# The first four token tiles taken one by one through w1, with w1 loaded in quarters

## The chip, the cores and the metric

The kernel runs on one core of one Trainium2 chip. The metric is device time in microseconds (us): the median of several executions. The record lists the span and the mean granted clock of every run (the granted clock is the share of TensorE's full clock that the profile shows as granted: 1.00 from 28.0 to 31.4 us before the change, 0.50 there after it), and of each kernel one execution's whole trace is kept. In the profile PE is TensorE, PEld its weight loads, DVE VectorE, ACT ScalarE, POOL GpSimd, and SP the engine that issues most DMAs. Times of lines in a trace count from the start of the span, which is about 2 us shorter than the device time (1514.3 against 1516.2 us before the change).

Ratios are the mean time of one kernel's fast runs over that of the other's fast runs of the same rounds, so they are not quite the ratios of the medians quoted here.

## The reference

```python
def reference(A_x, ..., B_w1, B_w2, B_w3, B_w4):        # cut
    def _B_ref(x, w1, w2, w3, w4):
        h = _gelu(_layernorm(x, axis=-1) @ w1)          # <- the stage that was changed
        ... four shifts of h along the tokens ...
        hs = concatenate([g0, g1, g2, g3], axis=-1) @ w2
        x1 = x + hs
        return x1 + _gelu(_layernorm(x1, axis=-1) @ w3) @ w4
    x = A_x                                             # 2048 tokens x 1024, bf16
    xn = _layernorm(x, axis=-1)
    return x + _A_ref(xn, ...) + _B_ref(xn, ...)        # _A_ref: attention by segments of 32 tokens
```

There are 2048 tokens in 16 tiles of 128. w1 is 1024 x 1024; the kernel holds it as 8 slices of 128 rows, the slices of the contraction. Only the first 5% of the kernel's time is at stake here: layernorm, w1 and gelu.

## The kernel before

Each tile is loaded, its mean and variance are taken (VectorE, with a power on GpSimd), it is normalised into `xn2` (VectorE), transposed so that features lie on partitions (by TensorE for tiles 0 to 3, by DMA for the others), multiplied by w1 (TensorE) and put through gelu (ScalarE). Beside this, ScalarE normalises `x` itself in place (`normalise_x`), and TensorE then adds it up by segments (`seg_sums`) for the attention. In the timelines below ScalarE works through its queue in the order in which the program issues (before the change four normalisations from 24.53 us, and the gelus behind them from 29.07).

```python
load_x(0); load_x(1); load_w1(0)            # w1 in two halves of four slices
load_x(2); load_x(3); load_w1(4)
for n in range(4, 8): load_x(n)
...
warm(16)                                     # useless matmuls, 0.427 us apart until the granted clock became 1.0 at 7.03 us
ln_stats(0); ln_stats(1)
ln_apply(0); pe_trans(0); warm(2)
ln_apply(1); pe_trans(1)
normalise_x(0); normalise_x(1)
... (cut: PSUM for the first pair)
for co in range(KT): w1_first(co, range(4))  # tiles 0 and 1 together: 256 columns a matmul
... (cut: statistics of tiles 2 to 5)
for c0 in range(0, KT, 2):
    w1_first(c0, range(4, KT)); w1_first(c0 + 1, range(4, KT)); w1_first_out((c0, c0 + 1))
    if c0 in (0, 2): pe_trans(c0 // 2 + 2)
for g in range(1, NT // 2):                  # the other seven pairs
    ... (cut: statistics and DMA transposes of the next pair)
    stage1(g, range(4))
    if g == 1:
        seg_sums(0); seg_sums(1)
        normalise_x(2); normalise_x(3)
    for n in nxt: normalise_x(n)             # with g == 1: tiles 4 and 5
    stage1(g, range(4, KT))
    seg_sums(2 * g); seg_sums(2 * g + 1)     # wait for normalise_x of these tiles
```

I call two tiles taken together a pair; the third pair is tiles 4 and 5. A `psX` line in a trace is a segment sum.

## Time and profile before

| | before |
|---|---|
| device time, median of 6 | 1516.2 us (1516.06 to 1516.35) |
| TensorE busy, of a span of 1514.3 us | 1497.6 us |
| first w1 matmul | 10.72 us |
| third pair starts | 29.48 us |
| w2 starts | 73.81 us |
| last matmul ends, to end of span | 3.80 us |

Two lines of the page's first and fourth part: the busy time of each engine, then each engine's share of the chain of work that ended last.

```profile
PE 1497.6 (99%) x9456; PEld 793.3 (52%) x9582; DVE 660.3 (44%) x1553; ACT 452.8 (30%) x1251; POOL 235.0 (16%) x652
...
PE 95%; DVE 3%; ACT 1%; issue 1%; DMA 0%; DVEq 0%; ACTq 0%
```

TensorE is the limit nearly everywhere. What can be gained in the first stage is therefore the time in which TensorE has no useful work there. The timeline of TensorE before shows it. The columns are start, length of the group, engine, source line, operation, output<-inputs, shape and count; in brackets is the idle time before the group and what ended it.

```profile
1.47 6.36 PE L197 MATMUL psW<-fill 128*128 128x512 bf16 x16 [1.47 <-DVE fill L175]
7.91 0.62 PE L243 MATMUL psT<-c_ident_sb,xn 128*128 128x128 bf16 x8
8.36 0.59 PE L197 MATMUL psW<-fill 128*128 128x512 bf16 x2
9.54 0.62 PE L243 MATMUL psT<-c_ident_sb,xn 128*128 128x128 bf16 x8 [0.58 <-DVE xn L218]
10.72 4.71 PE L285 MATMUL ps<-xn2T,w_sb 128*128 128x256 bf16 x40 [0.56 <-DVE xn2T L246]
...
19.50 1.03 PE L285 MATMUL ps<-xn2T,w_sb 128*128 128x256 bf16 x8 [0.96 <-ACT hT_all L290]
20.37 3.66 PE L258 MATMUL ps<-xn2T,w_sb 128*128 128x256 bf16 x32
...
27.75 0.54 PE L253 MATMUL psX<-c_segone_sb,x 128*128 128x4 bf16 x16
29.48 7.15 PE L258 MATMUL ps<-xn2T,w_sb 128*128 128x256 bf16 x64 [1.19 <-ACT hT_all L260]
```

Useful work begins at 10.72 us, because the first pair needs two tiles normalised, transposed and copied. Small holes follow, the last one before the third pair. From 29.48 us on TensorE never waits until w2 at 73.81. So the place to watch is the start of the third pair: what moves it moves the whole kernel. ScalarE's timeline shows why that last hole is there:

```profile
24.53 4.63 ACT L235 ACTIVATE x<-x,nm,lnst 128x1024 bf16<-128x1024 bf16 x4
29.07 1.17 ACT L260 ACTIVATE hT_all<-ps 128x256 bf16<-128x256 f32 x4
```

Four normalisations stand in ScalarE's queue ahead of gelus. TensorE's wait of 1.19 us before the third pair ended with the output of such a gelu (`hT_all`, L260), which reads the PSUM tile that TensorE wrote its sums to.

### The profile page before, as it was taken

What the parts mean: (1) busy time and instruction counts of PE and PEld (TensorE: products, weight loads), DVE (VectorE), ACT (ScalarE), POOL (GpSimd) and SP (SyncE); (2) the same over time, 40 slices, a digit from 0 to 9 for tenths busy, and PEclk for the clock granted to TensorE, in tenths of its full rate; (3) what the DMA queues carried; (4) which work ended last, traced back from release to release, by engine and by line L of the source; (5) the groups of instructions that cost most, each with busy time, mean ns of one, the idle gap of its engine ahead of it and who ended that gap; (6) DMA issues with size and microseconds to landing.
All of it is one profiled execution on the core that took longest, in us unless ns stands there. A gap on an engine that the chain in (4) does not pass through costs nothing.

```text
span 1514.3 us, 23917 instructions
## 1 busy us (share of the span) xinstructions
PE 1497.6 (99%) x9456; PEld 793.3 (52%) x9582; DVE 660.3 (44%) x1553; ACT 452.8 (30%) x1251; POOL 235.0 (16%) x652
## 2 busy tenths in 40 slices
PE   8999999999999999999999999999999999999998
PEld 6844444444444466666544554444444544454446
DVE  8284010010110226666622857731767640676653
ACT  5633202103012034454401344310433420334320
POOL 4142110111110211121210111110111110111100
PEclk9999999999999999999999999999999999999999
DMA  7699553553122545574522454421464431344211
GB/s 199 158 246 291 218 188 98 180 173 135 63 91 46 191 151 170 157 206 141 180 70 82 140 167 140 154 87 52 138 169 144 140 117 56 118 140 140 94 36 38
DMA packets 191029, 208.38 MB, mean 138 GB/s; under 512 B 51192, under 2 KB 158856, under 8 KB 190912
## 3 DMA queue, kind: packets, MB, share of 16 engines
q1 hardware_dynamic: 183664, 182.49, 40.2%
q0 software_dynamic: 7248, 24.31, 4.1%
q8 instruction: 77, 1.26, 0.4%
q14 instruction: 40, 0.33, 0.1%
HBM read 170.07 MB, written 25.17 MB: 129 GB/s over the span
## 4 chain that ended last, share of the span: by engine, by line
PE 95%; DVE 3%; ACT 1%; issue 1%; DMA 0%; DVEq 0%; ACTq 0%
PE psP L754 15%; PE psQ L582 14%; PE psK L598 14%; PE psV L605 14%; PE ps L517 13%; PE ps L535 13%; PE ps L339 4%; PE ps L258 3%; PE psO L657 2%; PE psS L627 2%; PE psM L614 1%; PE psY L776 1%; PE psvb L399 1%; PE psG L408 1%; PE ps L285 0%
## 5 line engine op out<-in xcount | busy, mean ns | idle before, releaser
L754 PE MATMUL psP<-wo_sb,oX 128*128 128x512 bf16 (+1 forms) x1036 | 221.7, 372 | 1.1
L631 ACT ACTIVATE ET<-psS 32x132 f32<-32x132 f32 x512 | 138.7, 271 | 188.8 <-PE psS L627 183.1
L535 PE MATMUL ps<-w,hT_all 128*128 128x512 bf16 x874 | 193.7, 379 | 1.2
L598 PE MATMUL psK<-xT,w 128*128 128x512 bf16 x747 | 176.3, 379 | 1.1
L582 PE MATMUL psQ<-xT,w 128*128 128x512 bf16 x750 | 175.9, 379 | 1.1
L605 PE MATMUL psV<-w,xT 128*128 128x512 bf16 x745 | 175.0, 379 | 1.0
L598 PEld LDWEIGHTS <-w 128*128 128x128 bf16 x1280 | 121.3, 98 | 80.1
L754 PEld LDWEIGHTS <-oX 128*128 128x128 bf16 x1056 | 102.8, 98 | 115.5
L582 PEld LDWEIGHTS <-w 128*128 128x128 bf16 x1024 | 96.9, 98 | 105.4 <-issue 1.3
L518 ACT ACTIVATE hT_all<-ps 128x512 bf16<-128x512 f32 x112 | 66.7, 597 | 283.9 <-PE ps L517 283.9
L535 PEld LDWEIGHTS <-hT_all 128*128 128x128 bf16 x896 | 87.0, 98 | 103.9
L665 ACT CAST oTm<-psO 128x16 bf16<-128x16 f32 x128 | 22.9, 179 | 366.1 <-DVE oX L661 366.1
L633 DVE STREAM_TRANSPOSE EQ<-ET 128x128 f32<-128x128 f32 x128 | 39.8, 311 | 165.6 <-ACT ET L631 165.2
L589 DVE TENSOR_TENSOR Q<-psQ,QM 128x512 bf16<-128x512 f32 (+1 forms) x128 | 85.2, 678 | 61.4 <-ACT Q L588 43.2
L605 PEld LDWEIGHTS <-xT 128*128 128x128 bf16 x768 | 72.1, 98 | 73.4
L648 POOL TENSOR_TENSOR BD<-ET,c_segone_sb 128x16 bf16<-128x16 f32 x128 | 33.7, 263 | 491.8 <-ACT ET L631 491.8
L517 PE MATMUL ps<-xn3T,w3a 128*128 128x512 bf16 x448 | 97.7, 379 | 0.0
L517 PE MATMUL ps<-xn3T,w3b 128*128 128x512 bf16 x448 | 97.7, 379 | 0.0
L646 DVE TENSOR_TENSOR BD<-PT,c_segone_sb 128x512 bf16<-128x512 bf16 x128 | 90.0, 703 | 4.4
L760 DVE TENSOR_TENSOR ot<-psP,Rt 128x512 bf16<-128x512 f32 (+1 forms) x33 | 22.2, 674 | 155.4 <-PE psP L754 155.4
L661 DVE TENSOR_TENSOR oX<-psO,VM 128x512 bf16<-128x512 f32 (+1 forms) x128 | 86.3, 674 | 7.2 <-PE psO L657 7.2
L599 ACT CAST K<-psK 128x512 bf16<-128x512 f32 (+1 forms) x160 | 78.5, 506 | 33.0 <-PE psK L598 32.4
(157 smaller groups left out, 1541.5 us busy)
## 6 DMA issues: line engine op xcount, KB each, us to landing
w<-in_A_Wq_dram SPq DMA_DIRECT2D x32, 1024.0 KB, 5.7
w<-in_A_Wk_dram SPq DMA_DIRECT2D x32, 1024.0 KB, 5.7
w<-in_A_Wv_dram SPq DMA_DIRECT2D x32, 1024.0 KB, 5.7
R_scratch<-x POOLq DMA_DIRECT2D x16, 512.0 KB, 4.1
R<-R_scratch SPq DMA_DIRECT2D x16, 512.0 KB, 7.8
chunk<-in_A_Wv_dram SPq DMA_DIRECT2D x8, 1024.0 KB, 6.3
R_scratch<-R POOLq DMA_DIRECT2D x16, 512.0 KB, 6.2
chunk<-in_A_Wo_dram SPq DMA_DIRECT2D x8, 1024.0 KB, 6.2
```

The costliest lines, as they stand in the source:

```text
L517: nc.tensor.matmul(ps[:], w3[:, k, (f % FH) * P:(f % FH + 1) * P], xn3Ts[tb][:, :, k, :], start=(k == 0), stop=(k == KT - 1))
L518: nc.scalar.activation(h3T[:, f, :], ps[:], ACTF.Gelu_apprx_tanh)
L535: nc.tensor.matmul(ps[:], h3T[:, f, j * P:(j + 1) * P], w4t[f // 4][:, f % 4, ch * 512:(ch + 1) * 512], start=(f == 0), stop=(f == FT - 1))
L582: nc.tensor.matmul(ps[:], w[:, k, hh * P:(hh + 1) * P], s.xm[:, k, 0:512], start=(k == 0), stop=(k == KT - 1))
L589: nc.vector.tensor_tensor(q3[:, j0:16, 0:SEG], p3_[:, j0:16, :], QM[:, 4 * s.hg + hh, z + j0:z + 16].unsqueeze(2).to_broadcast((P, 16 - j0 ...
L598: nc.tensor.matmul(ps[:, 0:c], w[:, k, hh * P:(hh + 1) * P], s.xm[:, k, h2 * c:(h2 + 1) * c], start=(k == 0), stop=(k == KT - 1))
L599: nc.scalar.copy(s.K[:, hh, h2 * c:(h2 + 1) * c], ps[:, 0:c])
L605: nc.tensor.matmul(ps[:], s.xm[:, k, m * P:(m + 1) * P], w[:, k, :], start=(k == 0), stop=(k == KT - 1))
L631: nc.scalar.activation(ET[q, :, :], ps[q, :, W * j:W * (j + 1)], ACTF.Exp, scale=SCALE)
L646: nc.vector.tensor_tensor(B4[:, :, :, 0:SEG], PT[:].unsqueeze(2).to_broadcast((P, 4, 4, SEG)), so.unsqueeze(3).to_broadcast((P, 4, 4, SEG) ...
L661: nc.vector.tensor_tensor(oX[:, hsl(s.hg), m * P:(m + 1) * P].rearrange("p h (j i) -> p h j i", i=SEG)[:, :, j0:4, :], p4[:, :, j0:4, 0:SE ...
L754: nc.tensor.matmul(ps[:, 0:w], oX[:, h, m * P:(m + 1) * P], wo_sb[:, h, cc], start=(h == 0), stop=(h == H - 1))
```

## The change

The intent: start w1 as soon as one tile and the first slices of w1 are there, and fill the early holes. w1 comes in four loads of two slices. Tile 0 runs with the slices outermost, so each slice is used as it lands. Tiles 0 to 3 go one at a time, with 128 columns a matmul. The statistics of tiles 1 and 2 are taken in halves around the normalisation of the tile before. All copies of transposed tiles go to ScalarE. The loop over pairs starts at the third.

```diff
             def load_w1(k0):
-                nc.sync.dma_start(w1_sb[:, k0:k0 + 4, :], w1_v[:, k0:k0 + 4, :])
+                nc.sync.dma_start(w1_sb[:, k0:k0 + 2, :], w1_v[:, k0:k0 + 2, :])
             load_x(0)
             load_x(1)
             load_w1(0)
+            load_w1(2)
             load_x(2)
-            load_x(3)
             load_w1(4)
-            for n in range(4, 8):
+            load_w1(6)
+            for n in range(3, 8):
                 load_x(n)
# ... cut: ln_half, and the copies of pe_trans all to ScalarE
-            warm(16)
+            warm(12)
             ln_stats(0)
-            ln_stats(1)
+            ln_half(1, 0)
             ln_apply(0)
             pe_trans(0)
-            warm(2)
+            ln_half(1, 1)
+            w1_first(range(5))
+            ln_half(2, 0)
             ln_apply(1)
             pe_trans(1)
# ... cut: the first pair's code, removed
+            w1_first(range(5, KT))
+            for b in range(2):
+                gelu4(0, b, first[:, b, :, :])
+            ln_half(2, 1)
+            ln_apply(2)
+            single(1, 0)
+            pe_trans(2)
+            normalise_x(0)
+            single(1, 1)
+            ln_stats(3)
+            ln_stats(4)
+            ln_apply(3)
+            single(2, 0)
+            pe_trans(3)
+            normalise_x(1)
+            single(2, 1)
+            ln_stats(5)
+            ln_apply(4)
+            dma_trans(4)
+            single(3, 0)
+            seg_sums(0)
+            seg_sums(1)
+            ln_stats(6)
+            ln_apply(5)
+            dma_trans(5)
+            single(3, 1)
+            for n in range(2, 6):
+                normalise_x(n)
+            seg_sums(2)
+            seg_sums(3)
-            for g in range(1, NT // 2):
+            for g in range(2, NT // 2):
# ... cut
```

`single(n, b)` is one tile's product with one half of w1's columns: 32 matmuls of 128 columns.

More of the change, by code (lines that the diff above doesn't have):

```diff
@@ L197, in warm, with ln_half @@
                     nc.tensor.matmul(ps[:], fill[:, 0:P], fill[:], start=(i == 0), stop=(i == c - 1))
-            def ln_stats(n):
-                st = ring.tile([P, 2, 6], F32, tag="st")
-                for c in range(2):
-                    nc.vector.bn_stats(st[:, c, :], xts[n][:, c * 512:(c + 1) * 512])
-                nc.vector.bn_aggr(lnst[:, n, 0:2], st[:])
-                ab = ring.tile([P, 2], F32, tag="ab")
+            sts = {}
+            def ln_half(n, c):
+                if c == 0:
+                    sts[n] = ring.tile([P, 2, 6], F32, tag="st", name="st")
+                nc.vector.bn_stats(sts[n][:, c, :], xts[n][:, c * 512:(c + 1) * 512])
+                if c == 0:
+                    return
+                nc.vector.bn_aggr(lnst[:, n, 0:2], sts.pop(n)[:])
+                ab = ring.tile([P, 2], F32, tag="ab", name="ab")
                 nc.vector.tensor_scalar(ab[:, 0:1], lnst[:, n, 1:2], EPS, None, op0=ALU.add)
@@ L207, in ln_stats @@
                 nc.gpsimd.tensor_tensor(lnst[:, n, 2:4], ab[:], neghalf[:], op=ALU.pow)
+            def ln_stats(n):
+                ln_half(n, 0)
+                ln_half(n, 1)
             xn2Ts = {}
@@ L243, in pe_trans @@
                         nc.tensor.matmul(p3_[:, k, :], xn2[:, (4 * h + k) * P:(4 * h + k + 1) * P], ident[:], start=True, stop=True)
-                    dst = xn2Ts[n // 2][:, n % 2, 4 * h:4 * h + 4, :]
-                    if h == 0 and n < 2:
-                        nc.vector.tensor_copy(dst, p3_)
-                    else:
-                        nc.scalar.copy(dst, p3_)
+                    for q in range(0, 4, 2 if n == 0 else 4):
+                        w = 2 if n == 0 else 4
+                        nc.scalar.copy(xn2Ts[n // 2][:, n % 2, 4 * h + q:4 * h + q + w, :], p3_[:, q:q + w, :])
             def seg_sums(n):
@@ L264, in stage1, with w1_first @@
                     w1_part(g, co, mm_tile("ps1")[:, 0:256], range(KT))
-            warm(16)
+            first = aux_tile([P, 2, 512], "B", "ps1")[:].rearrange("p b (c t) -> p b c t", c=4)
+            def w1_first(ks):
+                for k in ks:
+                    for co in range(KT):
+                        nc.tensor.matmul(first[:, co // 4, co % 4, :], w1_sb[:, k, co * P:(co + 1) * P], xn2Ts[0][:, 0, k, :],
+                                         start=(k == 0 and co % 4 == 0), stop=(k == KT - 1), skip_group_check=True)
@@ new lines, in gelu4, with single @@
+            def gelu4(n, b, ps):
+                nc.scalar.activation(hTB[:, 4 * b:4 * b + 4, 2 + n * P:2 + n * P + P], ps, ACTF.Gelu_apprx_tanh)
+            def single(n, b):
+                ps = mm_tile("ps1")[:].rearrange("p (c t) -> p c t", c=4)
+                for c in range(4):
+                    co = 4 * b + c
+                    for k in range(KT):
+                        nc.tensor.matmul(ps[:, c, :], w1_sb[:, k, co * P:(co + 1) * P], xn2Ts[n // 2][:, n % 2, k, :], start=(k == 0), stop=(k == KT - 1))
+                gelu4(n, b, ps)
@@ L267 @@
+            warm(12)
             ln_stats(0)
-            ln_stats(1)
+            ln_half(1, 0)
             ln_apply(0)
             pe_trans(0)
-            warm(2)
+            ln_half(1, 1)
+            w1_first(range(5))
+            load_segone()
+            load_eye9()
+            ln_half(2, 0)
             ln_apply(1)
             pe_trans(1)
-            normalise_x(0)
-            normalise_x(1)
-            load_segone()
-            load_eye9()
-            first = []
-            for tag in "AB":
-                t = aux_tile([P, 2, 512], tag, "ps1")
-                first += [t[:, c // 2, (c % 2) * 256:(c % 2 + 1) * 256] for c in range(4)]
@@ L283, in w1_first @@
-            def w1_first(co, ks):
-                for k in ks:
-                    nc.tensor.matmul(first[co], w1_sb[:, k, co * P:(co + 1) * P], xn2Ts[0][:, :, k, :], start=(k == 0 and co % 2 == 0),
-                                     stop=(k == KT - 1), skip_group_check=True)
-            def w1_first_out(c):
-                for co in c:
-                    nc.scalar.activation(hTB[:, co, 2:258], first[co], ACTF.Gelu_apprx_tanh)
-            for co in range(KT):
-                w1_first(co, range(4))
@@ L294 @@
-            ln_stats(2)
-            ln_stats(3)
-            for n in (2, 3):
-                ln_apply(n)
-            ln_stats(4)
-            ln_stats(5)
-            for c0 in range(0, KT, 2):
-                w1_first(c0, range(4, KT))
-                w1_first(c0 + 1, range(4, KT))
-                w1_first_out((c0, c0 + 1))
-                if c0 in (0, 2):
-                    pe_trans(c0 // 2 + 2)
-            for g in range(1, NT // 2):
+            w1_first(range(5, KT))
+            for b in range(2):
+                gelu4(0, b, first[:, b, :, :])
@@ L307 @@
+            ln_apply(5)
[6 more added lines that the diff above has]
+            for g in range(2, NT // 2):
                 nxt = [n for n in (2 * g + 2, 2 * g + 3) if n < NT]
                 for n in nxt:
-                    if 5 < n + 1 < NT:
+                    if 6 < n + 1 < NT:
                         ln_stats(n + 1)
@@ L313 @@
                 stage1(g, range(4))
-                if g == 1:
-                    seg_sums(0)
-                    seg_sums(1)
-                    normalise_x(2)
-                    normalise_x(3)
                 for n in nxt:
```

## The prediction

> **What bounds the kernel.** TensorE: 1497.6 of 1514.3 us busy, 95% of the chain of waits. The change touches only the first stage (layernorm, transposition, w1, gelu). In the TensorE timeline w1 starts at 10.72 us; the third pair starts at 29.48 us and from there it runs unbroken to w2 at 73.81. So the time moves as the start of the third pair (tiles 4 and 5), now 29.48 us, moves.
>
> **Before, up to 29.48.** 10.72 us lead-in; 128 matmuls of 256 columns at 0.109 us start to start = 14.0; transposes of tiles 2 and 3 (0.45 each) and four segment sums (0.2 each), 1.7; holes of 3.1: about 0.3 for the second half of w1, 0.4 and 1.1 for ScalarE evacuations, and 1.2 before the third pair, where ScalarE runs four normalisations (4.6 us) ahead of gelus.
>
> **What the change does.**
> 1. Statistics split: VectorE normalises tile 0 at about 6.5 instead of 7.31; transposes at 7.1 instead of 7.9.
> 2. Tile 0 no longer waits for tile 1, and w1 comes in quarters. The landings show the first half of w1 complete between 6.9 us (fastest DMA engine) and 10.22 (slowest), and about 0.68 us per 256 KB. Estimate for the slowest engine: quarters at 8.9, 10.2, 12.2 and 13.6 us. So w1 starts near 8.9, 1.8 us earlier, but waits about 0.5 and 1.1 us for quarters two and three; tile 0 is done near 14.6.
> 3. 256 matmuls of 128 columns replace 128 of 256. Transposes of that width run 0.056 us start to start, with weight loads hidden, so +0.4 us in all. [...]
> 4. Tiles 1 to 3: from 14.6, six halves of 1.8, two transposes and two segment sums: near 26.7.
> 5. Then a new hole: the gelu of tile 3's second half (0.5) and normalisations of tiles 2 and 3 (1.18 each) run on ScalarE in order before the segment sums of tiles 2 and 3, which TensorE must do before the third pair. About 3.2 us, against 1.2 before. The third pair starts near 30.
>
> **Sum.** -1.8 (start) +0.4 (narrow matmuls) +0.45 (one more transposition after the start) +1.7 (holes 4.8 instead of 3.1) = +0.7 us. Shaded, since the quarters may land earlier. Predicted 1516.5 us, 80% range 1514.3 to 1518.3. Chances: faster by over 2% 0.01, within 2% 0.98, slower 0.01.
>
> **What would show it.** w1 starting at 8.5 to 9.2 us, with DMA of w1 ending the idle time; DMA waits inside tile 0; narrow matmuls 0.056 us apart; a hole near 3 us before the segment sums of tiles 2 and 3, ended by ScalarE's normalisation; the third pair at 29 to 31 us; 44.3 us more to w2.
>
> **What would make it wrong.** (a) Landing: if quarters arrive a microsecond earlier, tiles 0 to 3 move up and time falls to about 1515. (b) The clock. The granted clock became 1.0 at 7.03 us; warm-up matmuls before it ran 0.427 us apart. With 12 instead of 16 warm-up matmuls (ending near 6.6) [...] tile 0 runs at half clock, costing 1 to 2 us. (c) Normalisation of tile 1 held up behind tile 2's first statistics, which wait for x. (d) The transposed tile 5 landing after 30 us.

-1.8 + 0.4 + 0.45 + 1.7 is +0.75 us, put there as +0.7.

## The result, and the profile after

The changed kernel took 1516.68 us (median of 6, 1515.47 to 1517.32), the kernel before 1516.2. The ratio is 1.0002, with a 95% interval of 0.9989 to 1.0015: the same. One thing stands out: the kernel before varies by 0.3 us from run to run, the changed one by 1.9.

| | before | after |
|---|---|---|
| first w1 matmul | 10.72 | 8.10 |
| third pair starts | 29.48 | 27.90 |
| w2 starts | 73.81 | 73.89 |
| from third pair to w2 | 44.33 | 45.99 |
| last matmul ends, to end of span | 3.80 | 4.29 |
| span | 1514.3 | 1515.1 |

TensorE's busy time and its share of the chain, from the page after:

```profile
PE 1504.7 (99%) x9704; PEld 795.4 (52%) x9704; DVE 658.8 (43%) x1551; ACT 453.7 (30%) x1247; POOL 235.1 (16%) x652
...
PE 97%; DVE 1%; ACT 1%; DMA 0%; issue 0%; SPq 0%; ACTq 0%; DVEq 0%
```

TensorE's timeline after, for the same stretch:

```profile
1.47 5.30 PE L198 MATMUL psW<-fill 128*128 128x512 bf16 x12 [1.47 <-DVE fill L175]
7.04 0.82 PE L252 MATMUL psT<-c_ident_sb,xn 128*128 128x128 bf16 x8 [0.27 <-DVE xn L227]
8.10 1.95 PE L278 MATMUL ps<-xn2T,w_sb 128*128 128x128 bf16 x32 [0.24 <-ACT xn2T L255]
10.30 0.62 PE L278 MATMUL ps<-xn2T,w_sb 128*128 128x128 bf16 x8 [0.26 <-DMA w_sb<-in_B_w_dram]
...
12.56 1.95 PE L289 MATMUL ps<-xn2T,w_sb 128*128 128x128 bf16 x32
14.35 0.61 PE L252 MATMUL psT<-c_ident_sb,xn 128*128 128x128 bf16 x8
...
22.79 1.95 PE L289 MATMUL ps<-xn2T,w_sb 128*128 128x128 bf16 x32
26.55 0.35 PE L260 MATMUL psX<-c_segone_sb,x 128*128 128x4 bf16 x8 [1.81 <-ACT x L244]
27.68 0.35 PE L260 MATMUL psX<-c_segone_sb,x 128*128 128x4 bf16 x8 [0.78 <-ACT x L244]
27.90 8.81 PE L265 MATMUL ps<-xn2T,w_sb 128*128 128x256 bf16 x64
36.55 0.54 PE L260 MATMUL psX<-c_segone_sb,x 128*128 128x4 bf16 x16
```

The early half does what was intended: w1 starts 2.62 us earlier, and but for one short wait for w1, at 10.30, TensorE runs without a break until 24.6. A half of a tile takes 1.79 us (12.56 to 14.35), 0.056 us a matmul. Then comes a hole of 1.81 and 0.78 us, ended by `x`, the output of ScalarE's normalisation. And the third pair, 64 matmuls, takes 8.81 us instead of 7.15. ScalarE's timeline shows where the hole comes from:

```profile
24.78 0.60 ACT L282 ACTIVATE hT_all<-ps 128x512 bf16<-128x512 f32 x1 [1.42 <-PE ps L289]
25.27 4.62 ACT L244 ACTIVATE x<-x,nm,lnst 128x1024 bf16<-128x1024 bf16 x4
```

ScalarE sat idle for 1.42 us, waiting for the matmuls of tile 3. Only behind tile 3's gelu did it find the normalisations of tiles 2 to 5 in its queue, and TensorE could not do the segment sums of tiles 2 and 3 before them. The normalisations could have run before, in ScalarE's idle time; the first experiment tests this.

The slow third pair has another cause. The view by stretches has, after each engine's busy time and count, the granted clock of TensorE, the DMA share and GB/s:

```profile
24.60:28.00 3.40, 0.81 (x20) 0.58 (x18) 3.20 (x8) 3.22 (x4) 1.30 (x3) 1.00 1.07 267
28.00:31.40 3.40, 3.40 (x19) 2.35 (x16) 3.19 (x11) 2.33 (x5) 1.18 (x2) 0.50 1.14 116
31.40:34.80 3.40, 3.40 (x33) 3.04 (x31) 2.45 (x7) 2.31 (x5) 1.31 (x3) 1.00 0.96 249
```

From 28.0 to 31.4 us the granted clock is 0.50. Matmuls of 256 columns start 0.213 us apart there instead of 0.109, and 19 are counted in that stretch instead of the 33 of the next. In the kernel before, the same stretch has the full clock:

```profile
28.00:31.40 3.40, 2.21 (x30) 1.95 (x28) 2.83 (x8) 2.79 (x9) 1.50 (x4) 1.00 1.15 230
```

That makes up the 1.66 us between 45.99 and 44.33. So the sum of this trace is: third pair 1.58 us earlier, lower clock 1.66 us, w2 0.08 us later. Behind w2, 0.25 us appear until the last matmul and 0.49 us after it. The 0.25 is of the size of the scatter: from w2 to the last matmul's end it is 1436.69 us before, and 1436.93 to 1437.18 in four executions of the changed kernel.

### The profile page after: what moved, and what is told of

It reads as the page before. It is cut to its first block, busy times and chain, and to the rows that moved or that the text cites. A ratio compares the mean times of both kernels' runs of the same rounds, so it can differ in the third digit from the quotient of the medians.

```text
span 1515.1 us, 24282 instructions
## 1 busy us (share of the span) xinstructions
PE 1504.7 (99%) x9704; PEld 795.4 (52%) x9704; DVE 658.8 (43%) x1551; ACT 453.7 (30%) x1247; POOL 235.1 (16%) x652
## 4 chain that ended last, share of the span: by engine, by line
PE 97%; DVE 1%; ACT 1%; DMA 0%; issue 0%; SPq 0%; ACTq 0%; DVEq 0%
PE psP L777 15%; PE psQ L605 14%; PE psK L621 14%; PE psV L628 14%; PE ps L540 13%; PE ps L558 13%; PE ps L362 4%; PE ps L265 3%; PE psO L680 2%; PE psS L650 2%; PE psM L637 1%; PE ps L289 1%; PE psY L799 1%; PE psvb L422 1%; PE psG L431 1%; DMA w_sb<-in_B_w_dram 0%
```

## The experiments

The theory was: the earlier start is worth 2 to 3 us at w2, and it is paid back by the hole in ScalarE's order and by the half clock that the hole brings. The rival: narrow matmuls, the extra ScalarE copies or the landings of w1 limit the stage, and the hole is only where slack shows. Four calls were made, each on one chip with its own runs of the kernel before, whose median was 1516.14 to 1516.16 us every time. Two single runs of it stood out, at 1522.15 us (the call of the first three experiments and of the second set of the changed kernel) and at 1525.07; they count in the ratios, and lower those by up to 0.0005.

### The normalisations earlier

```diff
             single(2, 1)
+            normalise_x(2)
             ln_stats(5)
# ... cut
             seg_sums(1)
+            normalise_x(3)
             ln_stats(6)
# ... cut
-            for n in range(2, 6):
+            for n in range(4, 6):
                 normalise_x(n)
```

Expected: 

> The changed kernel with one edit: the normalisations of tiles 2 and 3 are issued on ScalarE one step earlier each, into its idle stretches. Theory A (the gain of the earlier start is eaten by the 3.0 us hole before the segment sums of tiles 2 and 3, and by the half clock that follows it, 16 matmuls at 0.213 us instead of 0.109, 1.7 us): third pair starts near 25 us instead of 27.9, granted clock stays 1.0, w2 starts near 69.3 us instead of 73.89, time near 1512. Theory B (narrow matmuls, extra evacuations or w1 landings limit the stage, the hole is only where slack shows): another hole opens, w2 starts above 72.5, time above 1515.

Measured: correct, 1513.6 us (1512.47 to 1513.9), ratio 0.9978 (0.9966 to 0.9991). TensorE's timeline:

```profile
10.37 0.62 PE L278 MATMUL ps<-xn2T,w_sb 128*128 128x128 bf16 x8 [0.43 <-DMA w_sb<-in_B_w_dram]
...
22.86 1.95 PE L289 MATMUL ps<-xn2T,w_sb 128*128 128x128 bf16 x32
24.65 0.54 PE L260 MATMUL psX<-c_segone_sb,x 128*128 128x4 bf16 x16
25.27 7.16 PE L265 MATMUL ps<-xn2T,w_sb 128*128 128x256 bf16 x64
```

The granted clock stays at 1.00 where it had fallen:

```profile
28.00:31.40 3.40, 3.40 (x34) 3.04 (x32) 0.92 (x4) 3.13 (x6) 1.18 (x2) 1.00 0.74 98
```

The hole is gone, the third pair takes 7.16 us again, and w2 starts at 69.60 us. That is what theory A said in the trace. The traced run took 1512.76 us, and the median, 1513.6, is 1.6 us above the expected 1512. The trace had an early landing of w1 (see below); later landings in the other runs are the likely reason, which is not shown. Behind w2 this trace is 0.86 us longer than that of the kernel before (1441.35 against 1440.49 us to the end of the span), so not all that was gained at w2 comes out at the end. Theory B falls as the cause of this loss: no other hole opened, and w2 started far below its 72.5. I call this kernel the mended kernel.

### The hole filled with useless matmuls

```diff
+            warm(8)
             seg_sums(2)
             seg_sums(3)
```

Expected: 

> The changed kernel with eight useless 128x512 matmuls put into the hole (1.7 us of TensorE work), nothing else. The hole stays, TensorE is merely busy in it. Theory A1 (the fall of the granted clock to 0.5 at 28 us comes from the idle stretch): clock stays 1.0, third pair starts near 28 and w2 near 72.2 us, time about 1515.0, with a narrow spread like that of the kernel before. Theory A2 (the clock falls for another reason, or its fall costs nothing): time stays at 1516.7 with a spread near 2 us.

Measured: 1515.8 us (1515.25 to 1516.54). TensorE's timeline, then two stretches:

```profile
11.46 0.62 PE L278 MATMUL ps<-xn2T,w_sb 128*128 128x128 bf16 x8 [0.98 <-DMA w_sb<-in_B_w_dram]
...
25.74 1.89 PE L198 MATMUL psW<-fill 128*128 128x512 bf16 x7
27.72 0.35 PE L260 MATMUL psX<-c_segone_sb,x 128*128 128x4 bf16 x8
28.85 0.35 PE L260 MATMUL psX<-c_segone_sb,x 128*128 128x4 bf16 x8 [0.78 <-ACT x L244]
29.07 7.15 PE L265 MATMUL ps<-xn2T,w_sb 128*128 128x256 bf16 x64
```

```profile
24.60:28.00 3.40, 3.26 (x39) 2.09 (x37) 2.41 (x8) 2.06 (x3) 1.18 (x2) 1.00 1.11 286
28.00:31.40 3.40, 2.62 (x33) 2.31 (x31) 3.29 (x9) 3.40 (x7) 2.23 (x4) 1.00 1.38 177
```

The hole is still there, but TensorE is busy in it. The granted clock stays at 1.00, the third pair takes 7.15 us, and from its start to w2 it is 44.32 us, as in the kernel before. TensorE was busy for 3.26 of the 3.40 us up to 28.00, against 0.81 in the changed kernel. So the fall of the clock comes from the idle stretch (theory A1). The clock averages of the timed runs agree: five of the six are 1.000, in which a fall of 3.4 us has no room, against two of twelve in the changed kernel (see below). (The trace lacks the record of one of the eight added matmuls.) In this execution the third pair itself started late, at 29.07, because w1 landed late: the wait at 11.46 was at 10.30 in the trace of the changed kernel. Such landings are the likely reason, not shown, for the median's 0.8 us above the expected 1515.0. The narrow spread did not come: 1.3 us, against 0.3 in the kernel before. Against the changed kernel in the same call, the means of all runs are 1515.9 and 1517.2 us.

### The same cure in the kernel before

```diff
+                if c0 == 6:
+                    normalise_x(2)
                 w1_first_out((c0, c0 + 1))
+                if c0 == 6:
+                    normalise_x(3)
# ... cut, in the loop with g == 1:
-                    normalise_x(2)
-                    normalise_x(3)
```

Expected: 

> The kernel before with the same cure for its own hole of 1.2 us at 28.3 us: normalisations of tiles 2 and 3 issued earlier, between the gelus of the first pair. If that hole is ScalarE order alone: third pair near 28.3 instead of 29.48, time near 1515.1, and the change is then worth about 3 us beside a kernel that has no such hole either. If the earlier normalisations only delay gelus that TensorE waits for: no gain, 1516.2.

Measured: 1514.73 us (1514.7 to 1514.93), ratio 0.9987 (0.9974 to 0.9999). TensorE's timeline has no wait before the third pair any more:

```profile
27.68 0.54 PE L253 MATMUL psX<-c_segone_sb,x 128*128 128x4 bf16 x16
28.08 7.15 PE L258 MATMUL ps<-xn2T,w_sb 128*128 128x256 bf16 x64
```

The third pair started at 28.08 us and w2 at 72.40, which is 1.41 us earlier. So the kernel before had the same fault in a smaller size. The first of the two outcomes came true, with a time 0.4 us below the expected one. And the part of the gain that belongs to the change, mended kernel against mended kernel, is 1514.73 less 1513.6, about 1.1 us in the medians, not the 3 us that was expected there.

### The changed kernel looked at again

Expected: 

> The changed kernel once more, for its spread. [...] times spread over 1515.3 to 1517.4 again, and runs whose mean granted clock is 1.0 lie at the low end, those at 0.999 or 0.998 higher by 1 to 2 us. If the spread has another cause, clock and time do not go together.

Expected: 

> The changed kernel, one more look at the clock. The hole of 3 us before the segment sums of tiles 2 and 3 should be there again. [...] the clock falls to 0.5 for 3.4 us and about 16 matmuls run at 0.213 us. If the grant comes near 4 or 5.5 us instead, [...] there should be no fall, and w2 starts 1.7 us earlier at equal landings.

Expected: 

> As the look before: whether the clock falls after the hole should go with the time of the first grant, [...] and not with when w1 landed.

What can be tested: a fall after a first grant near 7.0 to 7.5 us, none after one near 4 or 5.5.

Measured: the second set of runs took 1517.57 us (1515.24 to 1519.12), so the spread is real, and wider than expected. In this set the mean granted clock of each run goes with its time, as the first of these texts had it: 1.000 at 1515.24 us, 0.999 at 1515.49, 1517.11 and 1518.03, 0.998 at 1518.30, 0.997 at 1519.12. In the first six runs it does so less: 1.000 at 1515.77, 0.998 at 1516.41, 0.999 at 1515.47 and at 1516.96 to 1517.32. A mean of 0.999 decides little, since the mended kernel's profiled run has it too, whose clock was 1.00 in all stretches that I looked at (5.30 to 15.50 and 24.00 to 37.70 us). But a mean that rounds to 1.000 leaves room for at most 1.5 us at half clock (an estimate: 2 x 0.0005 x 1515), and the falls in the traces last 3.41 us or more. So at least one run of each set had no such fall: the hole often brings it, and not always. The two single looks took 1518.58 and 1518.37 us (state unknown, since they are single). Their traces are what matters. The landing is that of the third quarter of w1: the trace has 16 landing records of each such DMA, which I put down to the 16 DMA engines of the page, and the first and the last of them are called the fastest and the slowest engine here.

| look | third quarter lands | fifth slice starts | third pair | first grant of the full clock | fall of the clock | w2 |
|---|---|---|---|---|---|---|
| first | 9.20 to 10.26 | 10.30 | 27.90 | 7.50 | 27.98 to 31.40 | 73.89 |
| again | 9.20 to 10.30 | 10.35 | 27.95 | 7.36 | 27.84 to 31.25 | 73.87 |
| third | 9.44 to 10.73 | 10.78 | 28.41 | 6.96 | 27.44 to 34.26 | 75.57 |
| fourth | 9.30 to 11.55 | 11.60 | 29.19 | 5.89 | 29.78 to 33.19 | 75.18 |

TensorE's timeline in the fourth look, and the stretch of the fall in the third:

```profile
9.56 1.07 PE L278 MATMUL ps<-xn2T,w_sb 128*128 128x128 bf16 x16 [0.22 <-DMA w_sb<-in_B_w_dram]
11.60 0.62 PE L278 MATMUL ps<-xn2T,w_sb 128*128 128x128 bf16 x8 [0.97 <-DMA w_sb<-in_B_w_dram]
...
29.19 8.81 PE L265 MATMUL ps<-xn2T,w_sb 128*128 128x256 bf16 x64
```

```profile
27.40:34.30 6.90, 6.13 (x36) 4.42 (x37) 5.90 (x15) 4.19 (x8) 3.37 (x6) 0.51 1.11 195
```

Two things vary. First, the landing: the fastest engine brings the third quarter within 0.3 us of the same time, the slowest within 1.3 us. From the fifth slice to the third pair it is 17.59 to 17.63 us in all four looks, so a late landing goes to the third pair in full. TensorE goes on 0.04 to 0.05 us after the slowest. Second, the clock fell in all four looks, in the third for 6.8 us. What I expected of the fourth look was wrong: its first grant came at 5.89 us, and the clock fell all the same.

By the table the falls begin 20.48, 20.48, 20.48 and 23.89 us after the first grant and last 3.42, 3.41, 6.82 and 3.41 us. How busy TensorE was before a fall is told by the view by stretches, which counts each matmul until its end. These are stretches of 3.40 us, with the granted clock of the stretch behind each:

| run | stretch | TensorE busy | clock behind it |
|---|---|---|---|
| changed kernel, first look | 24.60 to 28.00 | 0.81 us | 0.50 |
| changed kernel, third look | 24.00 to 27.40 | 1.58 us | 0.51 |
| w1 in halves (below) | 6.50 to 9.90 | 0.82 us | 0.50 |
| statistics whole (below) | 5.30 to 8.70 | 1.43 us | 0.50 |
| kernel before | 28.00 to 31.40 | 2.21 us | 1.00 |
| hole filled | 24.60 to 28.00 | 3.26 us | 1.00 |
| hole filled | 5.30 to 8.70 | 1.44 us | 1.00 |

So a stretch need not be idle to be followed by a fall. How little work it takes is not shown: the last row had no fall behind it with 1.44 us of work, the third look had one with 1.58. Nor is it shown why the clock stayed at half for 6.82 us in the third look, where the third pair took 9.99 us.

### Whole statistics, halves of w1, and a pair again, on the mended kernel

These three undo one part each, on the mended kernel, so that the hole and the fall after it are out of the way.

Statistics whole:

```diff
             ln_half(1, 0)
+            ln_half(1, 1)
             ln_apply(0)
             pe_trans(0)
-            ln_half(1, 1)
```

Expected: 

> The mended kernel with the statistics of tile 1 whole again before tile 0 is normalised. Tile 0 is normalised 0.87 us later (near 7.3), w1 starts near 8.95 instead of 8.0, but TensorE then no longer waits 0.4 to 0.6 us for the third quarter of w1: w2 near 70.0, that is 0.4 us later, hidden in the spread of the times. If the split were worth its full 0.87 us: w2 near 70.5.

Measured: 1514.15 us (1513.29 to 1514.6), 0.55 us above the mended kernel's median. It was run at another time. In its trace w1 started at 8.74 and the third pair at 26.77, 1.5 us later than the mended kernel's. Its lead-in ran at half clock:

```profile
5.30:8.70 3.40, 1.43 (x12) 0.70 (x11) 2.42 (x7) 0.39 (x2) 1.98 (x4) 1.00 0.84 292
8.70:12.10 3.40, 3.36 (x32) 3.36 (x32) 2.32 (x6) 0.81 (x3) 1.49 (x4) 0.50 1.05 403
```

With 12 warm-up matmuls and a later start, TensorE was busy for only 1.43 of the 3.40 us before. At 0.056 us a matmul, as in the trace of the changed kernel, the first 40 matmuls would have ended just behind the third quarter's landing at 10.79, and the transposition of tile 1 would have started at 11.3 instead of 12.56: by this estimate the clock is 1.3 us of the delay, and the rest is mostly landing. So w2 came at 71.09 instead of the 70.0 expected, and what the split is worth by itself this trace does not show; the medians differ by 0.55 us.

w1 in halves:

```diff
-                nc.sync.dma_start(w1_sb[:, k0:k0 + 2, :], w1_v[:, k0:k0 + 2, :])
+                nc.sync.dma_start(w1_sb[:, k0:k0 + 4, :], w1_v[:, k0:k0 + 4, :])
-            load_w1(2)
-            load_w1(6)
```

Expected: 

> The mended kernel with w1 in two loads of 512 rows instead of four of 256. The second half should land near 11.6 us (as the last quarter did), so the fifth slice starts there instead of at 10.3: w2 near 70.9 instead of 69.6. The number of DMAs is that of the kernel before, so the tail should be 3.8 us if the semaphore order sets it. Net about 0.8 us slower than the mended kernel, near 1514.2. If landings in quarters do not matter, w2 stays at 69.6.

Measured: 1515.31 us (1514.33 to 1515.78), 1.7 us above the mended kernel's median, though its end is 0.5 us shorter (see below). It was run at another time. TensorE's timeline:

```profile
10.22 4.08 PE L276 MATMUL ps<-xn2T,w_sb 128*128 128x128 bf16 x40 [2.52 <-DMA w_sb<-in_B_w_dram]
```

w1 started at 10.22 us after 2.52 us of waiting for it, w2 at 72.66, and the granted clock was 0.50 from 9.90 to 13.30 us, TensorE having been busy for 0.82 of the 3.40 us before. The first half, 512 rows in one piece, had landed on the slowest engine at 10.17 us here, and the second half at 13.63, not near the expected 11.6. The fifth slice started behind it, at 13.68. At 0.056 us a matmul the 32 matmuls before it would have ended near 12.0 and waited, so by this estimate the fall of the clock cost next to nothing here, and the loss is that of landings. The quarters were worth more than the 0.8 us expected, as far as one trace and medians tell.

Tiles 2 and 3 as a pair:

```diff
-            single(2, 0)
             pe_trans(3)
             normalise_x(1)
-            single(2, 1)
-            normalise_x(2)
# ... cut
-            single(3, 0)
+            stage1(1, range(4))
+            normalise_x(2)
# ... cut
-            single(3, 1)
+            stage1(1, range(4, KT))
```

Expected: 

> The mended kernel with tiles 2 and 3 taken together again, in 64 matmuls of 256 columns. If narrow matmuls are what costs (Theory B), this gains. By the trace they cost 0.17 us a pair (7.15 against 6.98), while the pair must wait for tile 3: its transposition can start near 17.0 and its copies end near 18.5, against 16.7 when tile 2 alone could start. So a hole near 1.9 us opens at 17 us and w2 starts near 71.3, 1.7 us later than with single tiles; time near 1515.2. A fall of the clock after that hole would add up to 1.7.

Measured: 1514.11 us (1513.43 to 1514.43). TensorE's timeline:

```profile
17.33 0.62 PE L252 MATMUL psT<-c_ident_sb,xn 128*128 128x128 bf16 x8 [0.24 <-DVE xn L227]
18.61 3.70 PE L265 MATMUL ps<-xn2T,w_sb 128*128 128x256 bf16 x32 [0.66 <-ACT xn2T L255]
...
27.06 7.15 PE L265 MATMUL ps<-xn2T,w_sb 128*128 128x256 bf16 x64 [0.47 <-DMA xn2T<-xn]
```

w2 starts at 71.38, as expected, and narrow matmuls are not what costs: from the fifth slice to the third pair it is 16.41 us, against 14.90 with single tiles. Some 0.6 of the 16.41 us is the wait for the transposed tile 5 in the last line, which has nothing to do with the width. In the medians the loss is only 0.5 us. The likely reason, argued and not shown, is that the pair's wait for tile 3 takes up late landings of w1, which single tiles pass on.

### The half microsecond at the end

Every trace of the changed kernel ends 4.29 to 4.30 us after the last matmul, of the kernel before 3.80. The DMAs of the sync queue use eight semaphores in turn, by whose updates the trace tells of their landing. The views leave semaphore instructions out; the trace has them. In the kernel before, with 271 DMAs on that queue, the last store is on the seventh and has landed at 1512.51 us; the closing waits, which go through the eight in order, pass the seventh at 1512.53 and the eighth at 1512.60. In the changed kernel, with 273, the last store is on the first and has landed at 1512.84; the waits pass the first at 1512.86, and the other seven, 0.07 to 0.1 us apart, until 1513.40. That is 0.48 us more behind the landing.

```diff
-                if 8 <= n < 12:
-                    kk = slice(2 * (n - 8), 2 * (n - 7))
+                if n in (9, 11):
+                    kk = slice(2 * (n - 9), 2 * (n - 7))
                     nc.sync.dma_start(w2_sb[:, kk, :], w2_v[:, kk, :])
```

Expected: 

> The mended kernel (normalisations of tiles 2 and 3 early) with the w2 load in two DMAs instead of four, so that the number of DMAs of the sync queue equals that of the kernel before. In the traces the time from the last matmul to the end is 3.80 us in the kernel before and 4.3 us in the changed one and all its variants so far. Theory T: the two extra w1 DMAs move the last store from the seventh to the first of eight DMA semaphores, which the closing waits take one after the other, so this tail should fall back to 3.8 us (0.5 us less), with all else as in the mended kernel: w2 near 69.6, time near 1513.0. Rival: the tail is longer for another reason (program length, fetches of instructions); then it stays at 4.3.

Measured: 1512.94 us (1512.73 to 1514.13), ratio 0.9978 (0.9965 to 0.9992). By the count of DMAs, 271 again, the last store is on the seventh semaphore, and the end takes 3.81 us. In the experiment with halves, which has two DMAs fewer for another reason, it is 3.80. So what theory T expected of the end came true. One thing was not as expected: w2 started at 71.32 in this trace. Late quarters explain 1.1 us (the fifth slice started at 11.47). The rest is a wait for a transposed tile, which was issued behind the w2 load that is now twice as large:

```profile
56.54 7.16 PE L265 MATMUL ps<-xn2T,w_sb 128*128 128x256 bf16 x64 [0.49 <-DMA xn2T<-xn]
```

In the next version, which leaves the w2 loads alone, this wait is absent: 44.34 us from the third pair to w2.

### Versions that beat both

The next version leaves the w2 loads alone, saves the two DMAs at w3 instead, and puts useless matmuls where TensorE waits in the lead-in:

```diff
-            warm(12)
+            warm(13)
# ... cut
             pe_trans(0)
+            warm(2)
# ... cut
-        for i in range(8, 16):
+        for k in (0, 2):
+            nc.sync.dma_start(w3b[:, k:k + 2, :], w3_v[:, k:k + 2, FH * P:2 * FH * P])
+        for i in range(12, 16):
             load_w3(i)
```

Expected: 

> The mended kernel with the tail shortened without touching the first stage (the first four rows of the second half of w3 in two DMAs instead of four, so the w2 loads keep their pace), and with one more warm-up matmul before and two after the transposes of tile 0, in time in which TensorE waits anyway. Third pair at 25.3 to 26.4 us, depending on when the slowest DMA engine lands the quarters of w1; no hole before w2 (44.3 us from third pair to w2); tail 3.8 us; time 1512.2 to 1513.3, below the kernel before by 3 to 4 us.

Measured: 1512.88 us (1512.69 to 1517.75; one run stands out, as does one of the kernel before on that chip, at 1525.07), ratio 0.998 (0.9959 to 1.0, an interval that reaches 1). The end takes 3.79 us. But a hole before the third pair has come back, ended by another releaser:

```profile
25.90 7.16 PE L265 MATMUL ps<-xn2T,w_sb 128*128 128x256 bf16 x64 [0.46 <-DMA xn2T<-xn]
```

The transposed tile 5 now comes too late. The last run normalises tile 5 before it takes the statistics of tile 6 (one line moved behind two others).

Expected: 

> The best version so far with tile 5 normalised before the statistics of tile 6 are taken, since there TensorE waited 0.6 us for the DMA transposition of tile 5 before the third pair. The transposition is issued near 23.1 instead of 24.3 us, so that hole (25.28 to 25.90) should close: third pair 0.6 us earlier at equal landings of w1, w2 near 69.6 to 70.7, tail 3.8 us, time 1512.0 to 1512.8. If another wait stands behind it (ScalarE), time stays at 1512.8.

Measured: 1513.38 us (1512.61 to 1513.43), ratio 0.9981 (0.9967 to 0.9994). The hole shrank to 0.17 us in the trace, but w1 landed late there (fifth slice at 11.31) and no gain in time can be told from the noise of landings. So there are four kernels with the same ratio of about 0.998: the early normalisations alone, and with them the three versions of the end. By their medians they are 2.6 to 3.3 us, some 0.2%, faster than the kernel before, and below the medians of the changed one too; all this is far below the 2% at which a kernel is called faster here. Which of the four is best the record does not show.

## Why the prediction was right or wrong

The time was right: 1516.5 was predicted and 1516.68 measured. That is in part luck, since the sum was right only because wrong terms cancelled: the start and the holes came out 2.2 us better than predicted, and the clock and what lies behind w2 cost 2.4 us that were not in the sum. The terms, from the two traces, in us at w2 and after:

| term | predicted | measured |
|---|---|---|
| w1 starts earlier | -1.8 | -2.62 |
| 256 narrow matmuls for 128 wide ones | +0.4 | +0.3 (256 x 0.0558 less 128 x 0.109) |
| one more transposition after the start | +0.45 | +0.45 |
| holes up to the third pair | +1.7 (3.1 to 4.8) | +0.3 (3.1 to 3.4) |
| half clock after the hole | 0 | +1.66 |
| behind w2 | 0 | +0.25 (of the size of the scatter) and +0.49 |
| sum | +0.7 | +0.8 |

- **The bound and the place to watch** were right: TensorE, and the start of the third pair. From there to w2 it is 44.3 us in every trace without a fall of the clock and without another wait.
- **The statistics split** was right in size: tile 0 was transposed at 7.04 us, predicted 7.1.
- **The landings** were wrong in this trace. Predicted for the slowest engine: 8.9, 10.2, 12.2 and 13.6 us. Measured: 6.60, 8.24, 10.26 and 11.62. So the start of w1 was released by ScalarE's copy of the transposed tile, at 8.10 us, and not by the DMA at 8.5 to 9.2. I took the slowest engine's lag from the trace before, in which it finished the first half of w1 at 10.22 us and the fastest at 6.87, as if it belonged to the load. It varies from run to run: the slowest engine's third quarter came between 10.26 and 11.55 in the four looks. The text named an early landing as its first risk, with a time near 1515; the landing came true, the time did not, because of the clock and of the end.
- **Narrow matmuls** were right: 0.056 us apart with a weight load to each. The prediction took the spacing from the transposes of 128 columns before the change (8 in 0.45 us); 32 of the narrow matmuls took 1.79 us after it, 55.8 ns each.
- **The hole in ScalarE's order** was right in cause and near in size: 3.2 us predicted, 1.81 + 0.78 = 2.59 us of idle time by the profile, which counts each matmul until its end; from start to start, less the time of the matmuls themselves, it is 2.9. Moving two normalisations removed it.
- **The clock** was foreseen for the lead-in (an assumption of mine) and not for the hole. This is the step that was missed: "About 3.2 us, against 1.2 before" priced the hole as lost time only. Its price was that and 1.66 us more, since TensorE came out of it at half clock. The hole, 1.81 and 0.78 us of idle time with a segment sum between, was followed by a fall in all four looks, though by their clock averages not in every timed run.
- **The end** was not in the prediction at all: 0.49 us, of which the closing waits behind the last store's landing show 0.48. Two DMAs fewer on that queue brought the end back to 3.80, 3.81 and 3.79 us in the three places tried (w1, w2 and w3).
- **The spread** was not predicted. Late landings and falls of the clock explain what the traces show, 73.87 to 75.57 us at w2. How much of each is in the other timed runs stays open, since no traces of them are kept; their clock averages say only that at least two of the twelve had no full fall.

## What to carry to other kernels

When a stage is brought forward on the engine that limits, look through the queues of the other engines for work that the next stage needs and that now stands behind something late. Here two lines moved in ScalarE's queue, with nothing else changed, turned no gain into one of 2.6 us. Price a hole in TensorE's work not only by its length, but also by the half clock that can follow it (here it followed stretches of 3.40 us in which TensorE was busy for 0.81 to 1.58 us, and cost 1.66 us in the first look; one stretch with 1.44 us had no fall behind it). A tighter start also passes on the jitter of the loads that a looser one took up (in the four looks the fifth slice started between 10.30 and 11.60 us, and the third pair 17.6 us behind it each time), so compare several traces before trusting one.
